# A transformer kernel with written-out queues: another order for all engines, other alternate engines, other PSUM banks

## The chip, the cores and the metric

The kernel runs on one core of a Trainium2 chip. A core has five engines with a queue each: TensorE (PE in the profile; its weight loads are listed apart as PEld), VectorE (DVE), ScalarE (ACT), GpSimd (POOL) and SyncE (SP), which here issues all DMAs. An engine takes the instructions of its queue strictly in order, and waits on semaphores for the others. The metric is the device time of one execution in microseconds (us).

## What is computed

Four layers in a row on `x` of 2048 tokens by 512 features: attention, MLP, attention, MLP, both attention layers with the same weights and both MLPs with the same weights. Cut to what matters:

```
def A(x, wqkv, wo):                      # 32 heads of 16, window of 256 tokens back
    q, k, v = split(x @ wqkv)
    scores = q @ k.T * 16 ** -0.5        # masked: 0 <= query - key < 256
    return (softmax(scores) @ v) @ wo
def B(x, w1, b1, w2, b2):                # 512 -> 1792 -> 512
    return gelu(x @ w1 + b1) @ w2 + b2
x = A_x
x = x + A(layernorm(x)); x = x + B(layernorm(x))
x = x + A(layernorm(x)); x = x + B(layernorm(x))
```

Data are bfloat16, products are accumulated in float32. `A_x` is the only input of tokens that is used.

## The kernel before

**Tiles.** Tokens are cut into 16 tiles of 128, `X` holds them in SBUF. The two passes through attention give 32 tiles and 16 blocks `b` of two tiles (blocks 0 to 7 are the first attention layer, 8 to 15 the second). The MLPs run in ten jobs (`JOBS`) of two or four tiles. Attention of block `b` needs K and V of blocks `b` and `b-1`, so the four layers overlap: while one block is in its softmax, matmuls of MLP jobs and of other blocks can run.

**One block.** `lnq` and `kv` take the layer norm of two tiles (statistics `bs`, `ba` on DVE, a power of -1/2 on POOL, the normalised `xn` on DVE), transpose it (by PE for the first tiles and the last two, else by DMA, steps `tx`), and project Q, K, V (`q`, `k`, `v`, line 653; `k` and `q` are 256 columns wide, `v` 512). The evacuations from PSUM are `qe`, `ke`, `ve`. V is also copied with its halves swapped by two DMAs a tile (`vs`). `attention(b)` then makes score steps `sc` (line 754): 10 of them for a full block, 5 for block 0 and for block 8. A score step writes four PSUM banks as two pairs, and each pair is read by one exponential of 128x1024 on ScalarE (`ex`, line 761), into `E` in SBUF. Parts of `E` are multiplied with a mask (`mk`, line 782, on DVE or POOL). Two value steps per block (`pv`, line 804) multiply `E` with V into a PSUM pair; DVE transposes it out (`od`, line 813), `rc` and `nm` normalise (line 821, on DVE or POOL), `ot` transposes back, four matmuls a tile give the output projection (`op`), and DVE adds it to `X` (`rs`, line 849).

**One MLP job.** 14 groups `m` (line 653) of four 512-column or 256-column matmuls; gelu on ScalarE, for eight groups straight from PSUM (`ge`, line 879), for six after DVE has added the bias (`gb`, line 871; `ga`, line 874). Then for each tile 14 steps `y` with W2 accumulate in one bank, POOL has prepared `X` plus bias (`xb`, line 887), and DVE adds (`ya`, line 894). In the last layer the tile is stored by a DMA (`out`).

**PSUM.** Eight banks of 128x512 float32. A group takes one bank or an even pair, holds it from its first matmul until the evacuation, and then frees it. With a score holding two pairs, the next score's banks, the value steps and all filler share what is left.

**What sets the order.** The program is a list of 3098 nodes (`_Plan.add`), each with its engine, what it reads and writes, which PSUM group it takes or frees, and for some an alternative engine. `_Plan.run` (line 393 on) then takes three written-out lists: `_ORDER` (line 167), a permutation of all nodes, from which each engine's queue is the subsequence of its nodes; `_ALT` (line 331), the nodes that run on their alternative engine; and `_BANKS` (line 343), the first bank of each of the 658 groups in the order in which they are taken. Semaphore waits are derived from the order afterwards (`_Sched.op`). Nothing else decides when something runs: no cost or due time is computed in the kernel. SP's queue is part of the order as well, so the place of each load, transpose and copy is in the list.

The node names in the text are the keys in the code; "score 4.6" is `sc4_6`, step 6 of block 4. 18 warm-up matmuls (`warm`) on zeros stand at the start.

Of the kernel before, what the change touches and what calls it, by code (L numbers as in the profile page):

```python
# [19 lines left out]
class _Sched:  # L20
# [147 lines left out]
    15, 34, 5, 0, 6, 14, 35, 7, 33, 28, 38, 29, 47, 8, 18, 23, 9, 36, 3, 26, 31, 10, 57, 37, 11, 22, 1, 40, 4, 24,  # L168
    2, 58, 59, 61, 17, 42, 62, 21, 60, 65, 41, 63, 19, 64, 68, 55, 32, 66, 107, 39, 69, 67, 20, 105, 50, 70, 3097,
    48, 30, 27, 53, 25, 106, 108, 71, 109, 49, 72, 110, 73, 16, 74, 114, 81, 75, 82, 111, 83, 84, 115, 85, 86, 116,  # L170
    112, 87, 88, 89, 113, 195, 153, 117, 127, 128, 151, 196, 129, 130, 154, 118, 152, 131, 119, 197, 155, 120, 156,
    98, 99, 100, 121, 12, 101, 90, 13, 102, 367, 91, 368, 104, 159, 92, 93, 157, 94, 103, 325, 76, 369, 199, 77,
    326, 95, 78, 200, 79, 370, 132, 80, 133, 96, 134, 135, 201, 323, 97, 203, 198, 137, 136, 158, 138, 205, 144,
    139, 202, 140, 145, 204, 141, 146, 160, 147, 122, 520, 217, 148, 123, 206, 124, 219, 143, 125, 208, 126, 46,
    218, 324, 43, 213, 209, 327, 328, 215, 166, 167, 168, 331, 169, 214, 207, 371, 176, 329, 177, 521, 373, 210,
    178, 330, 216, 179, 522, 171, 172, 180, 372, 161, 173, 211, 142, 174, 170, 56, 375, 220, 162, 376, 332, 163,
    164, 523, 175, 524, 221, 374, 377, 150, 212, 165, 149, 380, 378, 222, 188, 382, 189, 44, 190, 181, 45, 525,
    182, 381, 223, 385, 183, 224, 191, 386, 184, 384, 226, 225, 227, 54, 231, 232, 387, 379, 233, 526, 234, 383,
    333, 228, 185, 343, 388, 389, 334, 192, 229, 235, 344, 395, 194, 230, 335, 396, 345, 238, 346, 291, 390, 236,
    397, 239, 237, 347, 240, 336, 241, 348, 337, 349, 338, 242, 350, 244, 339, 243, 391, 399, 351, 401, 340, 341,  # L180
    352, 400, 245, 403, 342, 392, 402, 51, 353, 405, 52, 354, 355, 398, 356, 186, 360, 404, 357, 361, 362, 527,
    363, 393, 408, 364, 253, 409, 260, 261, 407, 254, 262, 410, 359, 413, 255, 246, 247, 415, 411, 256, 412, 257,
    248, 249, 250, 258, 414, 406, 564, 251, 273, 394, 274, 566, 263, 276, 416, 267, 268, 417, 565, 264, 270, 271,
    265, 277, 642, 285, 286, 423, 567, 418, 640, 275, 643, 528, 287, 529, 428, 272, 419, 282, 252, 283, 429, 288,
    259, 289, 641, 420, 308, 290, 309, 421, 424, 266, 310, 311, 279, 278, 644, 269, 422, 645, 284, 307, 280, 312,
    281, 313, 314, 315, 540, 425, 426, 568, 427, 541, 570, 316, 648, 542, 543, 649, 317, 569, 544, 318, 530, 531,
    319, 532, 187, 533, 572, 534, 193, 320, 574, 321, 646, 430, 431, 322, 647, 292, 573, 293, 294, 432, 577, 295,
    435, 579, 366, 576, 296, 545, 297, 436, 358, 571, 298, 433, 578, 546, 582, 434, 547, 437, 584, 548, 575, 550,
    438, 899, 551, 552, 650, 583, 553, 439, 651, 441, 652, 440, 653, 554, 900, 897, 585, 592, 654, 299, 549, 300,
    301, 593, 365, 302, 303, 304, 442, 581, 305, 594, 586, 535, 536, 898, 580, 596, 537, 306, 598, 538, 587, 901,  # L190
    539, 902, 597, 595, 600, 588, 557, 601, 660, 661, 662, 663, 599, 602, 605, 664, 558, 559, 607, 560, 655, 656,
    561, 457, 458, 606, 603, 610, 903, 657, 589, 658, 612, 904, 604, 453, 590, 459, 454, 476, 455, 477, 611, 485,
    486, 563, 609, 479, 591, 480, 482, 562, 613, 659, 470, 471, 483, 556, 905, 464, 465, 467, 478, 468, 484, 608,
    450, 460, 469, 461, 906, 451, 466, 446, 452, 447, 481, 443, 487, 448, 444, 473, 472, 462, 665, 474, 456, 614,
    666, 667, 445, 463, 615, 449, 475, 616, 684, 625, 626, 668, 617, 489, 686, 620, 618, 490, 491, 492, 685, 493,
    619, 621, 494, 669, 688, 687, 627, 690, 628, 622, 629, 495, 488, 623, 689, 496, 632, 692, 497, 694, 498, 624,
    691, 499, 500, 501, 630, 502, 693, 697, 504, 631, 505, 633, 1017, 506, 698, 507, 508, 634, 509, 1018, 510, 503,
    635, 699, 511, 702, 1019, 670, 512, 704, 700, 671, 672, 1020, 695, 673, 1021, 703, 674, 712, 696, 513, 514,
    701, 676, 714, 515, 706, 516, 517, 705, 518, 713, 519, 716, 638, 707, 717, 715, 718, 833, 720, 708, 721, 677,
    917, 1022, 918, 919, 709, 722, 920, 719, 710, 725, 921, 678, 727, 679, 680, 724, 681, 726, 730, 922, 636, 923,  # L200
    1023, 731, 912, 924, 728, 1024, 913, 723, 914, 915, 732, 729, 925, 711, 941, 637, 943, 734, 907, 908, 909, 733,
    910, 916, 926, 555, 735, 942, 639, 1025, 911, 736, 945, 934, 946, 935, 675, 737, 947, 738, 683, 949, 1026, 936,
# [763 lines left out]
```

## Time and profile before

| | us |
|---|---|
| median of 3 runs | 442.67 (442.11 to 443.06) |
| span of the profiled execution, first to last instruction | 442.4 |
| PE busy | 416.1 (94%) |
| ACT busy | 386.4 (87%) |
| DVE busy | 341.0 (77%) |
| POOL busy | 212.7 (48%) |
| mean DMA rate over the span | 53 GB/s |

The profile shows one execution; its device time is not listed apart from its span. In the rows of a stretch of time stand its bounds and length, then busy us and number of instructions of PE, PEld, DVE, ACT and POOL, the granted clock of TensorE (1.00 is full), the mean busy share of the 16 DMA engines and GB/s. In a row of waits stand the waiting engine and its line, the engine and line waited for, us in total, times, and the longest. In a row of a group, after the bar: us busy, mean ns of one, then idle us before it and what ended it. In a row of the order of time: start, us, engine, line, operation, output and inputs, count, and in brackets the idle time just before and who ended it. Matmuls are pipelined, so their durations overlap; starts give the rate.

### The profile page before, as it was taken

What the parts mean: (1) busy time and instruction counts of PE and PEld (TensorE: products, weight loads), DVE (VectorE), ACT (ScalarE), POOL (GpSimd) and SP (SyncE); (2) the same over time, 40 slices, a digit from 0 to 9 for tenths busy, and PEclk for the clock granted to TensorE, in tenths of its full rate; (3) what the DMA queues carried; (4) which work ended last, traced back from release to release, by engine and by line L of the source; (5) the groups of instructions that cost most, each with busy time, mean ns of one, the idle gap of its engine ahead of it and who ended that gap; (6) DMA issues with size and microseconds to landing.
All of it is one profiled execution on the core that took longest, in us unless ns stands there. A gap on an engine that the chain in (4) does not pass through costs nothing.

```text
span 442.4 us, 16864 instructions
## 1 busy us (share of the span) xinstructions
PE 416.1 (94%) x7523; PEld 233.2 (53%) x7593; DVE 341.0 (77%) x638; ACT 386.4 (87%) x458; POOL 212.7 (48%) x236
## 2 busy tenths in 40 slices
PE   8997999988789997999999999999999999999997
PEld 4555657544444563554455455455555464444675
DVE  7997789788785599967698868877888576746762
ACT  4997999999889999889899989999897988999533
POOL 3566344363442674711575454634728165804411
PEclk9999999999899999999999999999999999999999
DMA  7686422004101012121031021100421014003002
GB/s 234 184 209 185 87 64 45 20 10 69 39 3 25 16 34 56 28 46 24 4 65 31 1 57 26 34 20 10 69 39 20 20 39 105 14 1 81 15 0 73
DMA packets 48116, 23.25 MB, mean 53 GB/s; under 512 B 33196, under 2 KB 48044, under 8 KB 48044
## 3 DMA queue, kind: packets, MB, share of 16 engines
q1 hardware_dynamic: 48044, 22.17, 22.2%
q8 instruction: 60, 0.98, 0.9%
q14 instruction: 12, 0.10, 0.1%
HBM read 8.00 MB, written 2.10 MB: 23 GB/s over the span
## 4 chain that ended last, share of the span: by engine, by line
PE 79%; ACT 11%; DVE 6%; issue 2%; DMA 1%; DVEq 0%
PE ps L653 59%; PE ps L754 9%; PE ps L804 9%; ACT E L761 9%; DVE OD L813 1%; PE ps L539 1%; DVE stat L599 1%; DVE X L849 1%; DMA xnTB<-xn 1%; ACT gT L879 1%; ACT L879 1%; DVE KT L687 1%; DVE E L782 0%; PE ps L639 0%; ACT QT L590 0%
## 5 line engine op out<-in xcount | busy, mean ns | idle before, releaser
L761 ACT ACTIVATE E<-ps 128x1024 bf16<-128x1024 f32 x300 | 284.2, 1033 | 28.7 <-PE ps L754 28.0
L782 POOL TENSOR_TENSOR E<-E,mask 128x512 bf16<-128x512 bf16 (+2 forms) x111 | 120.9, 1106 | 91.3 <-ACT E L761 91.0
L653 PE MATMUL ps<-W_sb,gT 128*128 128x512 bf16 (+1 forms) x434 | 112.2, 373 | 3.2 <-issue 2.2
L653 PE MATMUL ps<-xnTB,W_sb 128*128 128x512 bf16 (+1 forms) x541 | 107.8, 336 | 3.4 <-issue 1.8
L653 PEld LDWEIGHTS ps<-xnTB,W_sb 128*128 128x128 bf16 x560 | 52.0, 98 | 42.9 <-issue 4.1
L653 PE MATMUL ps<-xnTA,Wqkv_sb 128*128 128x256 bf16 x512 | 70.7, 273 | 0.9 <-ACT E L761 0.4
L782 DVE TENSOR_TENSOR E<-E,mask 128x512 bf16<-128x512 bf16 (+2 forms) x125 | 60.1, 500 | 13.3 <-ACT E L761 12.9
L754 PE MATMUL ps<-QT,KT 32*128 32x128 bf16 (+3 forms) x1920 | 60.3, 231 | 9.8 <-ACT E L761 5.6
L653 PEld LDWEIGHTS ps<-W_sb,gT 128*128 128x128 bf16 x462 | 41.2, 98 | 41.1 <-issue 3.6
L754 PEld LDWEIGHTS ps<-QT,KT 32*128 32x128 bf16 x1920 | 28.5, 92 | 59.1 <-ACT E L761 34.9
L653 PEld LDWEIGHTS ps<-xnTA,Wqkv_sb 128*128 128x128 bf16 x512 | 47.4, 98 | 20.2 <-issue 2.9
L813 DVE STREAM_TRANSPOSE OD<-ps 128x1024 f32<-128x1024 f32 x32 | 39.9, 1246 | 21.3 <-PE ps L804 20.7
L887 POOL TENSOR_TENSOR Xb<-X,b2all 128x512 f32<-128x512 bf16 x32 | 37.7, 1180 | 34.3 <-DVE X L894 33.9
L879 ACT ACTIVATE gT<-ps,b1T 128x512 bf16<-128x512 f32 (+1 forms) x80 | 42.6, 609 | 9.5 <-PE ps L653 9.4
L804 PE MATMUL ps<-E,Va 64*17 64x128 bf16 (+3 forms) x1920 | 44.3, 234 | 1.9 <-issue 0.8
L821 POOL TENSOR_TENSOR Nb<-OD,Rc 128x512 bf16<-128x512 f32 x25 | 26.4, 1058 | 38.7 <-DVE Rc L817 29.8
L804 PE MATMUL ps<-E,Vs 64*17 64x128 bf16 (+3 forms) x1920 | 44.9, 234 | 0.0
L599 DVE BATCH_NORM_STATS2 stat<-X 128x6 f32<-128x512 bf16 x64 | 42.9, 679 | 0.5
L804 PEld LDWEIGHTS ps<-E,Va 64*17 64x17 bf16 x1920 | 37.2, 85 | 11.6 <-issue 9.0
L871 DVE TENSOR_SCALAR gT<-ps,b1T 128x512 bf16<-128x512 f32 (+1 forms) x60 | 36.8, 632 | 6.6 <-PE ps L653 6.2
L687 DVE TENSOR_TENSOR KT<-ps,parmask 128x1024 bf16<-128x1024 f32 x32 | 38.7, 1211 | 3.6 <-PE ps L653 3.6
L804 PEld LDWEIGHTS ps<-E,Vs 64*17 64x17 bf16 x1920 | 38.0, 85 | 0.2
(55 smaller groups left out, 348.8 us busy)
## 6 DMA issues: line engine op xcount, KB each, us to landing
Vs<-Va SPq DMA_DIRECT2D x64, 68.0 KB, 2.0
W_sb<-in_B_w_dram SPq DMA_DIRECT2D x4, 512.0 KB, 4.8
out_dram<-X SPq DMA_DIRECT2D x15, 128.0 KB, 1.8
X<-in_A_x_dram SPq DMA_DIRECT2D x3, 512.0 KB
Wqkv_sb<-in_A_wqkv_dram SPq DMA_DIRECT2D x4, 256.0 KB, 4.5
W_sb<-in_B_w_dram SPq DMA_DIRECT2D x2, 384.0 KB, 7.1
W_sb<-in_B_w_dram SPq DMA_DIRECT2D x1, 768.0 KB, 5.0
Wqkv_sb<-in_A_wqkv_dram SPq DMA_DIRECT2D x1, 512.0 KB, 6.7
```

The costliest lines, as they stand in the source:

```text
L599: add("dve", lambda e, B, t=t, k6=k6: e.bn_stats(stat6[:, k6, :], X[:, t, :]), reads=["X%d" % t], writes=["st%d" % k6], key="bs%d" % (k + j))
L653: r = e.matmul(ps[:, B[g][0], cols], lhsT, rhs, start=st, stop=sp)
L687: add("dve", lambda e, B, g=g, i=i: e.tensor_tensor(out=KT[:, kb, 2 * i : 2 * i + 2].rearrange("p c m a q -> p a (c m) q"), in0=ps[:, B[g] ...
L754: x = e.matmul(ps[:, bk[r], o : o + n], KT[rows, kb, c, m].rearrange("p a q -> p (a q)"), QT[rows, c, q : q + n], start=True, stop=True)
L761: add("act", lambda e, B, g_=g_, gi=gi: e.activation(E[:, 2 * gi : 2 * gi + 2, e0 : e0 + 512], ps[:, B[g_][0] : B[g_][0] + 2, :], AF.Exp, ...
L782: fn = lambda e, B: e.tensor_tensor(out=Ew, in0=Ew, in1=Mw, op=ALU.mult)
L804: x = e.matmul(ps[32 * r : 32 * r + VW, B[g][par], c % 2 * 2 * P + lo : c % 2 * 2 * P + hi], V[rows, (2 * b + m // 2) % VR, c * HC + 2 * r ...
L813: add("dve", lambda e, B: e.transpose(OD[:, s].rearrange("p a c q -> p (a c q)"), ps[:, B[g][0] : B[g][0] + 2, :]), reads=["ps:" + g], wri ...
L821: return e.tensor_tensor(out=Nb[:, s, :].rearrange("p (k a d) -> p a k d", a=2, d=Dh), in0=sums[:, :, :, 0:Dh], in1=rc[:, :, :, None].to_b ...
L871: add("dve", lambda e, B, g=g, fc=fc: e.tensor_scalar(out=gT[:, fc, c0 : c0 + M], in0=ps[:, B[g][0], 0:M], scalar1=b1T[:, fc : fc + 1], sc ...
L879: add("act", lambda e, B, g=g, fc=fc: e.activation(gT[:, fc, c0 : c0 + M], ps[:, B[g][0], 0:M], AF.Gelu_apprx_tanh, bias=b1T[:, fc : fc + ...
L887: add("pool", lambda e, B, t=t, xs=xs: e.tensor_tensor(out=Xb[:, xs, :], in0=X[:, t, :], in1=b2all[:], op=ALU.add), reads=["X%d" % t, "b2a ...
```

## The change

The three lists are replaced; no other line changes. The nodes, their instructions, their dependencies and the buffers in SBUF are the same.

- `_ORDER`: a new permutation. PE's queue has the same 1629 nodes; 372 of them stand more than 10 places away from where they were, most by a few places within the same stage. Three short warm-up matmuls now stand among the scores of blocks 0 and 1. Ten steps `y` more stand behind the score step 7.8, and one step `q`. The queues of ScalarE, DVE, POOL and SP are reordered likewise. SP's begins with x tiles 0, 1, 4-7, then K weights, x tiles 2-3, Q weights, the bias; before, with x tiles 0, 1, 2-3, the bias, then Q, K weights.
- `_ALT`: 164 nodes instead of 172; 104 are in both. Masks on DVE and POOL: 133 and 103 (before 125 and 111). Normalisations `nm`: 11 and 21 (before 7 and 25). Evacuations on ScalarE: 15 `qe`, 12 `ve`, 4 `te` (before 13, 10, 3). The small addition before the power: 9 on DVE, 22 on POOL (before 10, 21).
- `_BANKS`: 658 entries again; 529 groups lie in another bank than before. Pairs are at even banks in both.

ScalarE's table is switched as often as before (19 loads in each queue).

```diff
 _ORDER = [
-    15, 34, 5, 0, 6, 14, 35, 7, 33, 28, 38, 29, 47, 8, 18, 23, 9, 36, 3, 26, 31, 10, 57, 37, 11, 22, 1, 40, 4, 24,
...
-    3080, 3053, 3054, 2734, 3055, 3056, 3057, 2906, 3058, 3059, 3096, 3060, 3061, 2387, 3062, 2923, 3063,
+    34, 15, 8, 5, 35, 14, 16, 6, 42, 24, 37, 19, 17, 38, 0, 9, 21, 57, 36, 1, 28, 10, 47, 4, 58, 7, 11, 22, 61, 59,
...
+    3080, 3059, 3060, 3095, 3061, 2923, 3062, 3096, 3063,
 ]
 
 _ALT = [
-    67, 70, 75, 102, 109, 116, 121, 148, 165, 170, 185, 192, 198, 202, 211, 216, 337, 342, 370, 374, 378, 384, 389,
...
+    67, 70, 75, 113, 116, 121, 148, 165, 185, 192, 198, 202, 207, 211, 327, 337, 364, 370, 374, 378, 379, 384, 388,
...
 ]
 
 _BANKS = [
-    0, 1, 0, 1, 0, 2, 3, 2, 3, 5, 7, 0, 6, 5, 3, 2, 5, 4, 2, 4, 2, 3, 3, 5, 0, 1, 2, 6, 1, 5, 2, 4, 6, 1, 0, 2, 4, 6,
...
+    1, 0, 1, 0, 1, 0, 7, 0, 1, 0, 1, 1, 0, 7, 1, 0, 1, 7, 6, 1, 2, 3, 2, 0, 4, 3, 2, 7, 0, 2, 4, 5, 2, 6, 0, 1, 4, 2,
...
 ]
```

361 rows, old and new, of tables (_ALT, _BANKS, _ORDER) are left out of this document.

## The prediction

> **What bounds the kernel now.** I read the page first (busy shares and the slices), then the busy times in six stretches cut at score steps, then the waits, then the order of time around the worst place. A score step is the block of matmuls on line 754 that fills two PSUM pairs; ScalarE empties each pair with one exponential (line 761). I write "score 4.6" for step 6 of attention block 4.
>
> ```profile
> span 442.4 us, 16864 instructions
> PE 416.1 (94%) x7523; PEld 233.2 (53%) x7593; DVE 341.0 (77%) x638; ACT 386.4 (87%) x458; POOL 212.7 (48%) x236
> PEclk9999999999899999999999999999999999999999
> ```
> ```profile
> 0.00:10.69 10.69, 9.18 (x61) 5.36 (x62) 8.27 (x22) 5.53 (x9) 4.03 (x15) 1.00 0.77 229
> 10.69:55.72 45.03, 40.91 (x795) 26.39 (x802) 38.92 (x73) 41.48 (x54) 24.92 (x30) 1.00 0.66 167
> 55.72:81.69 25.97, 25.60 (x520) 17.74 (x523) 22.10 (x44) 24.74 (x34) 10.86 (x11) 1.00 0.26 54
> 81.69:141.85 60.16, 52.48 (x983) 27.38 (x992) 47.75 (x91) 55.27 (x63) 27.29 (x31) 0.97 0.15 25
> 141.85:204.68 62.83, 58.60 (x1187) 32.42 (x1197) 50.75 (x98) 57.81 (x65) 32.49 (x34) 1.00 0.17 34
> 204.68:440.08 235.40, 229.31 (x3987) 123.91 (x4028) 173.17 (x312) 201.60 (x237) 113.13 (x118) 1.00 0.16 34
> ```
> ```profile
> PEld ps L754 <- ACT E L761: 34.9, 80, 1.5
> ACT E L761 <- PE ps L754: 28.0, 50, 1.8
> ```
> The columns are the stretch, its length, then PE, PEld, DVE, ACT and POOL busy, the granted clock, DMA share and GB/s. The cuts are scores 0.0, 2.1, 3.0, 5.3 and 7.8. From 204.68 on PE is busy 229.31 of 235.40: nothing is left there but PE's own work, and ScalarE has 34 us to spare. Between 10.69 and 204.68 (193.99 us) PE is busy 177.59 and ScalarE 179.30. Neither is full; they wait for each other by turns, as the two wait rows say: a score waits for the exponential that frees its banks, then the exponential for the score. What a new order can win lies in these 16.4 us of idle PE, and is decided by how evenly other matmuls are laid between the scores.
>
> **The prices.**
> ```profile
> 200.25 0.81 PE L653 MATMUL ps<-xnTB,W_sb 128*128 128x512 bf16 x3
> 200.90 0.59 PE L653 MATMUL ps<-W_sb,gT 128*128 128x512 bf16 x2
> 201.33 0.82 PE L653 MATMUL ps<-xnTA,Wqkv_sb 128*128 128x256 bf16 x6
> 201.99 0.38 PE L653 MATMUL ps<-xnTB,W_sb 128*128 128x512 bf16 x1
> 204.68 0.40 PE L754 MATMUL ps<-QT,KT 32*128 32x192 bf16 x12
> 205.01 1.68 PE L653 MATMUL ps<-W_sb,gT 128*128 128x512 bf16 x7
> 206.63 0.40 PE L754 MATMUL ps<-QT,KT 32*128 32x256 bf16 x8
> ```
> ```profile
> 213.70 1.37 PE ps L804 x120
> L761 ACT ACTIVATE E<-ps 128x1024 bf16<-128x1024 f32 x300 | 284.2, 1033 | 28.7 <-PE ps L754 28.0
> L590 ACT ACTIVATE QT<-ps 128x512 bf16<-128x512 f32 x13 | 8.0, 613 | 1.6 <-PE ps L653 1.6
> ```
> Starts, not durations, give PE's rate: a 512-column matmul takes (200.90 - 200.25)/3 = 0.217, a 256-column one (201.99 - 201.33)/6 = 0.11, a score 205.01 - 204.68 = 0.33, and from 205.01 to 206.63 seven matmuls and the wait for the score take 1.62, so each score adds 0.10. A value step (line 804) takes 1.37. An exponential takes 284.2/300 = 0.95 in sequence (I use 0.94), a copy on ScalarE 0.61. Six fillers and a score are 1.64 + 0.10 against 1.88 for two exponentials: seven fillers match ScalarE, fewer leave PE waiting, more leave ScalarE waiting.
>
> **The change, part by part.**
>
> *Filler between scores.* With these prices I added, for each score step, the PE work since the score before and the ScalarE work up to its second exponential, and took the larger. In the list of before PE's work in the four stretches is 40.7, 25.8, 51.1 and 58.8, ScalarE's 43.1, 25.7, 55.7 and 58.2, and the larger parts sum to 45.4, 27.7, 60.2 and 63.7, together 197.0; the trace has 193.99, so the sum describes this kernel within 2%. In the new list PE has 41.5, 24.7, 51.1 and 56.9, ScalarE 41.9, 25.7, 55.1 and 58.8, and the larger parts sum to 44.3, 26.7, 57.6 and 63.9, together 192.5. That is 4.5 less. But the new list has laid ten steps of the second MLP product and a little more behind score 7.8, 2.3 us of PE work, where PE is the bound: net -2.2. That is one end. The other: were the eight banks deep enough to even out everything inside a stretch, only the larger total of each stretch would count, 183.4 before and 181.5 after: -1.9 + 2.3 = +0.4. The measured 193.99 lies 78% of the way from 183.4 to 197.0, so I take -2.2 + 0.22 x 2.6 = -1.6.
>
> *The hole at 113 us, and the clock.*
> ```profile
> 112.73 0.40 PE L754 MATMUL ps<-QT,KT 32*128 32x256 bf16 x8
> 114.38 0.40 PE L754 MATMUL ps<-QT,KT 32*128 32x256 bf16 x8 [1.25 <-ACT E L761]
> 116.21 0.40 PE L754 MATMUL ps<-QT,KT 32*128 32x192 bf16 x12 [0.46 <-ACT E L761]
> 116.79 2.32 PE ps L804 x125
> 121.30 1.02 ACT L761 ACTIVATE E<-ps 128x1024 bf16<-128x1024 f32 x1 [1.78 <-PE ps L754]
> ```
> ```profile
> 37.98:41.39 3.41, 2.03 (x29) 1.24 (x31) 2.50 (x3) 3.04 (x4) 1.02 (x1) 1.00 0.40 77
> 113.07:116.48 3.41, 1.70 (x32) 1.02 (x28) 3.08 (x7) 3.41 (x5) 0.26 (x1) 1.00 0.20 40
> 116.48:119.89 3.41, 2.90 (x138) 2.15 (x132) 0.70 (x1) 3.02 (x4) 1.21 (x2) 0.50 0.20 42
> ```
> Scores 4.5 (112.73) and 4.6 (114.38) have nothing between them. In the 3.41 us up to 116.48 PE is busy 1.70, and for the next 3.41 its clock is 0.50: the value step takes 2.32 where 1.37 is normal, and ScalarE stands for 1.78. The new list has five matmul steps ahead of score 4.6 and a value step ahead of 4.7, so this hole is closed. I price the lost half clock at 2.32 - 1.37 = 0.95 (ends: 0, if another hole takes its place, and 1.78) and take -0.95. [...]
>
> *The start.*
> ```profile
> 0.78 1.35 SPq L548 DMA_DIRECT2D X<-in_A_x_dram  x3
> X<-in_A_x_dram SPq DMA_DIRECT2D x1, 256.0 KB, 2.9
> 6.00:7.00 1.00, 1.00 (x8) 0.46 (x6) 0.97 (x2) 0.91 (x2) 0.00 (x0) 1.00 1.15 342
> 5.69 1.28 DVE L599 BATCH_NORM_STATS2 stat<-X 128x6 f32<-128x512 bf16 x2
> 9.40 1.22 DVE L687 TENSOR_TENSOR KT<-ps,parmask 128x1024 bf16<-128x1024 f32 x1 [0.38 <-PE ps L653]
> ```
> On SP's queue the 256 KB load of x tiles 2 and 3 goes from third to fifth, behind 512 KB (tiles 4 to 7) and 256 KB of weights. At 342 GB/s these 768 KB are 2.3 us, so it lands near 7 instead of 1.7 + 2.9 = 4.6, and the statistics move from 5.69 to about 7.1. In the new DVE queue two more statistics (0.68 each, in the fence below) and both normalisations of that pair stand ahead of the first K evacuation, which goes from 9.40 to about 10.8: score 0.0 comes up to 1.35 later. But those two statistics (2 x 0.68 = 1.36) are then done, and DVE, busy 38.92 of the next 45.03, has them off its list. Ends 0 and +1.35; I take +0.5, nearer to the work than to the wait.
>
> *Engines exchanged.*
> ```profile
> L782 POOL TENSOR_TENSOR E<-E,mask 128x512 bf16<-128x512 bf16 (+2 forms) x111 | 120.9, 1106 | 91.3 <-ACT E L761 91.0
> L782 DVE TENSOR_TENSOR E<-E,mask 128x512 bf16<-128x512 bf16 (+2 forms) x125 | 60.1, 500 | 13.3 <-ACT E L761 12.9
> L821 POOL TENSOR_TENSOR Nb<-OD,Rc 128x512 bf16<-128x512 f32 x25 | 26.4, 1058 | 38.7 <-DVE Rc L817 29.8
> L599 DVE BATCH_NORM_STATS2 stat<-X 128x6 f32<-128x512 bf16 x64 | 42.9, 679 | 0.5
> ```
> Masks go from 111 to 103 on POOL, normalisations from 25 to 21, and ScalarE makes five more evacuations: POOL loses 8 x 1.1 + 4 x 1.06 = 13 us of 212.7; ScalarE gets 5 x 0.61 = 3.1, all of it behind 204.68, where it has 34 to spare; DVE gets 8 x 0.5 and four normalisations (0.75 each, an estimate at the rate of its other 512-wide work) and gives up five evacuations of 0.68 (estimated alike), about +3.5 of 341.0. I cost them at nothing: the cover is DVE's 12.4 idle us of 60.16 in the stretch where it gets most of it. Were that gone, up to +3.5.
>
> *The other DMAs, the tail.* The first two transposes for the MLP still follow all three W1 loads, with about as many bytes ahead; 0, with 0.5 either way. Behind the last score both lists hold PE work alone (29.6 and 30.3 us, inside the 2.3 above); the last output tile is the same: 0.
>
> Sum: -1.6 - 0.95 + 0.5 = -2.05. The profiled span is 442.4 and the median of the runs 442.67, so 0.27 lies outside the span or between executions; I leave it there: 442.67 - 2.05 = 440.6. Measurement tells this kernel from no change at about 0.2%, 0.9 us.
>
> **The rivals.**
>
> *Not faster: work pushed behind 204.68 is not bought back.* If ScalarE idles in the first stretches as it does now (193.99 - 179.30 = 14.7), score 7.8 comes only by its lower work sooner, 182.7 - 181.5 = 1.2, and then 2.3 us more PE work follows: +1.1, 443.8. For it: the two wait rows are a mutual lock that even filler need not loosen. Against: the sum of larger parts followed the trace. It decides as soon as less than 2.3 us are won before score 7.8.
>
> *Another hole halves the clock.* The new list has its emptiest place at scores 4.2 and 4.3: 0.33 + (0.33 + 4 x 0.217) = 1.53 of PE work in four exponentials, 3.76. The rows put the limit between 1.70 and 2.03 busy in 3.41, so if a window falls there, the 0.95 is paid as now: 441.6. [...]
>
> *Nothing moves.* The first score is late by the full 1.35, the mutual waits give -1.6, and a half clock is paid in some other place: 442.4, within 0.2%. For it: 768 KB stand ahead of x tiles 2 and 3. Against: DVE has work to put in the gap.
>
> **How the numbers follow.** Forecast 440.6: 0.38. Second hole 441.6: 0.14. No change: 0.18. Slower, 443.8: 0.30. Faster is the first two, 0.52. The likeliest one's own range is 439.0 (442.67 - 2.2 - 0.95 with no cost at the start is 439.5, less 0.5 from the other DMAs) to 441.6. The whole range goes from 437.8, 1.2 below that for stalls the sum does not count, to 444.4, the slower rival with half of the start's cost.
>
> **What would show it.** Score 7.8 should start near 200.3 (204.68 + 0.5 - 0.95 - 1.6 - 2.3) and the rest take 2.3 longer. Right: fewer than 80 waits of scores for exponentials, clock 1.00 around 105 to 125. Wrong: first score later than 12, score 7.8 after 202.4, a half-clock slice elsewhere, or PE idle above 6 us after score 7.8.

## The result: 3% slower, and the profile after

The changed kernel takes 455.96 us (455.68 to 456.53) beside 442.49 us (442.11 to 443.06) for the kernel before: 1.0308 times as long, 95% interval 1.0293 to 1.0323. The forecast was 440.6, the range 437.8 to 444.4. In this kernel's code every line number is 7 lower than before (the score is line 747, its exponential 754, the matmul helper 646, the value step 797); in the experiments' kernels numbers can be one higher again.

The page after, and the same six stretches cut at scores 0.0, 2.1, 3.0, 5.3 and 7.8:

```profile
span 454.1 us, 16925 instructions
...
PE 428.3 (94%) x7593; PEld 232.9 (51%) x7593; DVE 346.4 (76%) x644; ACT 389.6 (86%) x463; POOL 202.2 (45%) x225
...
PEclk9989999999899999899999999999999999999999
```
```profile
0.00:12.32 12.32, 9.19 (x57) 5.07 (x59) 9.02 (x22) 6.07 (x10) 4.20 (x16) 1.00 0.87 258
12.32:62.36 50.04, 44.13 (x814) 28.04 (x814) 40.40 (x76) 40.81 (x53) 26.98 (x30) 0.97 0.59 138
62.36:87.20 24.84, 24.84 (x509) 16.25 (x508) 21.89 (x41) 23.81 (x33) 11.22 (x10) 1.00 0.17 29
87.20:147.67 60.47, 53.91 (x996) 26.51 (x990) 49.08 (x94) 55.39 (x63) 23.18 (x28) 0.97 0.19 33
147.67:211.74 64.07, 59.21 (x1190) 31.66 (x1191) 51.63 (x94) 56.41 (x64) 32.76 (x35) 0.97 0.21 34
211.74:451.60 239.86, 237.03 (x4041) 125.39 (x4040) 174.17 (x321) 207.14 (x245) 103.85 (x108) 1.00 0.17 33
```

PE's busy times of before and after can't be subtracted: the profile of before holds 7523 of the 7593 matmuls, this one all. So the 416.1 of before is too low and the idle time that the prediction read from it too high. A kernel below that differs from before in two pieces alone, with all 7593 recorded, has PE busy 424.4 of the same span of 442.4; between its scores 0.0 and 7.8 PE idles 12.6, where the prediction read 16.4.

The waits, as the profile puts them down:

```profile
ACT E L754 <- PE ps L747: 32.4, 47, 3.3
PEld ps L747 <- ACT E L754: 30.9, 76, 1.1
...
PE ps L646 <- DMA xnTA<-xn: 4.5, 2, 2.6
...
PE ps L646 <- DMA xnTB<-xn: 3.2, 2, 2.3
...
PE ps L797 <- DMA Vs<-Va: 1.4, 1, 1.4
```

Scores wait a little less for exponentials (34.9 to 30.9), exponentials a little more for scores (28.0 to 32.4). New are PE's own waits for DMAs: before, the longest was 0.7. Four of them in the order of time, the last with the two issues that precede it on SP's queue:

```profile
26.28 2.13 PE L646 MATMUL ps<-xnTA,Wqkv_sb 128*128 128x256 bf16 x10 [2.62 <-DMA xnTA<-xn]
...
57.92 0.60 PE L646 MATMUL ps<-xnTA,Wqkv_sb 128*128 128x256 bf16 x4 [1.86 <-DMA xnTA<-xn]
...
127.17 0.81 PE L646 MATMUL ps<-xnTB,W_sb 128*128 128x512 bf16 x3 [2.27 <-DMA xnTB<-xn]
...
324.36 1.27 SPq L625 DMA_TRANSPOSE xnTB<-xn  x1
325.67 0.59 SPq L695 DMA_DIRECT2D Vs<-Va  x1
...
327.84 0.28 PE L797 MATMUL ps<-E,Va 64*17 64x256 bf16 x4 [1.36 <-DMA Vs<-Va]
```

The last is a V copy (`vs24_0`, one half of tile 24's swapped V). Its source was ready at 313.35, but it was issued at 325.67, because other steps stand ahead of it in SP's order, and landed 2 us later: the value step stood.

The wait rows miss cases in which the weight load ahead of a matmul did the waiting. So for every stretch of over 0.3 us in which PE stood, from 6 us on, I took the operands and bank releases that the next matmul needs and asked which came last. In us:

| what ended PE's idle time | before | after |
|---|---|---|
| ScalarE (exponentials, which free the scores' banks) | 6.2 | 2.8 |
| VectorE | 2.7 | 4.5 |
| the landing of a DMA | 0.6 | 11.8 |
| sum | 9.5 | 19.1 |

So the new order did loosen the waits it was predicted to loosen, by 3.4, and pays 11.2 for transfers that land too late. The sum rises by 9.6. By stretch, with the differences that the prediction's "larger parts" gave:

| stretch, up to score | predicted | measured | new waits for landings in it |
|---|---|---|---|
| 0.0 | +0.5 | +1.6 | 0.8 (first weights) |
| 2.1 | -1.1 | +5.0 | 2.6, 1.9 (transposes 4, 9), 1.1 (V copy 2) |
| 3.0 | -1.0 | -1.1 | none |
| 5.3 | -2.6 | +0.3 | 2.3 (transpose 39), 0.9 (V copy 7) |
| 7.8 | +0.2 | +1.2 | 0.9 (transpose 42) |
| end | +2.3 | +4.5 | 1.4 (V copy 24) |

In the one stretch without a late transfer the working is right to 0.1. That is a weak test, since by the prediction's own sums this stretch has 1.1 less of PE's work (25.8 to 24.7) and would be shorter by it in any case. The rest of the time is TensorE's clock: three windows at half clock, each behind a window in which PE was busy 0.71, 1.51 and 1.67 of 3.41.

```profile
23.10:26.51 3.41, 0.71 (x22) 0.33 (x11) 1.53 (x3) 2.60 (x3) 1.06 (x2) 1.00 0.37 78
26.51:29.92 3.41, 3.41 (x23) 1.91 (x21) 2.45 (x6) 0.91 (x1) 0.00 (x0) 0.50 0.86 267
111.84:115.25 3.41, 1.51 (x24) 0.46 (x16) 3.31 (x5) 3.07 (x4) 2.07 (x2) 1.00 0.54 86
115.25:118.66 3.41, 3.41 (x23) 1.05 (x26) 2.26 (x6) 2.75 (x3) 1.78 (x2) 0.50 0.43 76
180.11:183.52 3.41, 1.67 (x36) 0.60 (x34) 3.08 (x6) 3.41 (x4) 1.83 (x3) 1.00 0.46 77
183.52:186.93 3.41, 2.86 (x7) 0.89 (x7) 1.77 (x4) 2.03 (x3) 1.56 (x2) 0.50 0.45 92
```

A run's time is its span plus 1.8 us (454.1 and 455.93 here). The kernel before was run again 30 times: 27 runs at a granted clock of 0.999 or 1.00 have spans of 439.7 to 441.7, median 440.5, and three at 0.996 have 441.8 to 442.2. The profiled execution of 442.4, with its half-clock window at 116.48, is thus nearly 2 us slower than the usual one, and a window costs some 1.4. The account is then 9.6 of waits and three windows at 1.3, together 13.5, where the medians differ by 13.5. The 1.3 is chosen to close it, and lies beside the 1.4.

### The profile page after: what moved, and what is told of

It reads as the page before. It is cut to its first block, busy times and chain, and to the rows that moved or that the text cites. A ratio compares the mean times of both kernels' runs of the same rounds, so it can differ in the third digit from the quotient of the medians.

```text
span 454.1 us, 16925 instructions
## 1 busy us (share of the span) xinstructions
PE 428.3 (94%) x7593; PEld 232.9 (51%) x7593; DVE 346.4 (76%) x644; ACT 389.6 (86%) x463; POOL 202.2 (45%) x225
## 4 chain that ended last, share of the span: by engine, by line
PE 73%; ACT 9%; DMA 7%; DVE 7%; SPq 3%; issue 1%; POOL 0%; DVEq 0%
PE ps L646 57%; PE ps L747 8%; PE ps L797 8%; ACT E L754 7%; DMA xnTB<-xn 3%; DMA xnTA<-xn 2%; DVE E L775 2%; DVE stat L592 1%; DMA X<-in_A_x_dram 1%; SPq L695 1%; SPq L625 1%; DVE X L887 1%; ACT gT L872 1%; DVE X L842 1%; DVE Va L581 1%
## 5 line engine op out<-in xcount | busy, mean ns | idle before, releaser
L754 ACT ACTIVATE E<-ps 128x1024 bf16<-128x1024 f32 x300 | 284.4, 1036 | 33.7 <-PE ps L747 32.4
L775 POOL TENSOR_TENSOR E<-E,mask 128x512 bf16<-128x512 bf16 (+2 forms) x103 | 111.6, 1095 | 96.0 <-ACT E L754 95.8
L646 PE MATMUL ps<-xnTB,W_sb 128*128 128x512 bf16 (+1 forms) x560 | 115.7, 340 | 3.3 <-DMA xnTB<-xn 3.2
L646 PE MATMUL ps<-W_sb,gT 128*128 128x512 bf16 (+1 forms) x462 | 118.8, 374 | 0.0
L646 PE MATMUL ps<-xnTA,Wqkv_sb 128*128 128x256 bf16 x512 | 74.2, 277 | 5.5 <-DMA xnTA<-xn 4.5
L775 DVE TENSOR_TENSOR E<-E,mask 128x512 bf16<-128x512 bf16 (+2 forms) x133 | 65.3, 512 | 10.6 <-ACT E L754 10.2
L747 PEld LDWEIGHTS ps<-QT,KT 32*128 32x128 bf16 x1920 | 28.2, 93 | 54.8 <-ACT E L754 30.9
L797 PE MATMUL ps<-E,Va 64*17 64x128 bf16 (+3 forms) x1920 | 43.3, 230 | 5.8 <-DVE Va L581 1.6
L797 PE MATMUL ps<-E,Vs 64*17 64x128 bf16 (+3 forms) x1920 | 43.9, 230 | 0.0
L814 POOL TENSOR_TENSOR Nb<-OD,Rc 128x512 bf16<-128x512 f32 x21 | 22.5, 1072 | 43.6 <-DVE Rc L810 43.6
L646 PE MATMUL ps<-Wo_sb,OT 128*128 128x512 bf16 x128 | 40.6, 388 | 0.2 <-DVE OT L820 0.2
```

The lines of the kernel that those rows point to most:

```text
L646: r = e.matmul(ps[:, B[g][0], cols], lhsT, rhs, start=st, stop=sp)
L747: x = e.matmul(ps[:, bk[r], o : o + n], KT[rows, kb, c, m].rearrange("p a q -> p (a q)"), QT[rows, c, q : q + n], start=True, stop=True)
L754: add("act", lambda e, B, g_=g_, gi=gi: e.activation(E[:, 2 * gi : 2 * gi + 2, e0 : e0 + 512], ps[:, B[g_][0] : B[g_][0] + 2, :], AF.Exp, ...
L775: fn = lambda e, B: e.tensor_tensor(out=Ew, in0=Ew, in1=Mw, op=ALU.mult)
L797: x = e.matmul(ps[32 * r : 32 * r + VW, B[g][par], c % 2 * 2 * P + lo : c % 2 * 2 * P + hi], V[rows, (2 * b + m // 2) % VR, c * HC + 2 * r ...
L814: return e.tensor_tensor(out=Nb[:, s, :].rearrange("p (k a d) -> p a k d", a=2, d=Dh), in0=sums[:, :, :, 0:Dh], in1=rc[:, :, :, None].to_b ...
```

## The experiments

In the diffs OLD and NEW are the node lists of the kernel before and of the changed kernel. No experiment leaves any of the computation out; one makes a score step three times. Score times are starts, compared with the profiled execution of before.

### Which of the three lists

**New order and engines, other banks.** 500 of the 658 groups lie elsewhere, each chosen by how long a bank had been free.

```diff
 _BANKS = [
-    1, 0, 1, 0, 1, 0, 7, 0, 1, 0, 1, 1, 0, 7, 1, 0, 1, 7, 6, 1, 2, 3, 2, 0, 4, 3, 2, 7, 0, 2, 4, 5, 2, 6, 0, 1, 4, 2,
+    0, 1, 2, 3, 4, 5, 6, 7, 0, 1, 2, 3, 4, 5, 6, 0, 7, 1, 5, 2, 3, 6, 4, 0, 2, 7, 6, 4, 0, 2, 7, 6, 2, 4, 0, 1, 2, 6,
...
```

> The new order and the new alternate engines with another set of PSUM banks: 500 of 658 groups get another bank, chosen so that each takes the bank that has been free longest. If the banks cause the loss, the time moves by several us, toward 444 to 450. If late transfers and the start cause it, the banks are innocent: 456 within 1.5, the gaps of PE near 24, 58, 114 and 127 us stand where they were, and score 1.1 starts at 28.3 within 0.5.

Measured 462.31 (460.52 to 464.1), ratio 1.0447. PE's waits for exponentials rise from 2.8 to 9.3. The banks of the change are better than these by 6 us. This is outside both ranges, and score 1.1 comes at 25.18 and not at 28.3, so neither theory is confirmed; one worse set does not show that the banks of the change cost nothing. It gives no sign that they do.

**New order and banks, the engines of before.**

```diff
 _ALT = [
-    67, 70, 75, 113, 116, 121, 148, 165, 185, 192, 198, 202, 207, 211, 327, 337, 364, 370, 374, 378, 379, 384, 388,
+    67, 70, 75, 102, 109, 116, 121, 148, 165, 170, 185, 192, 198, 202, 211, 216, 337, 342, 370, 374, 378, 384, 389,
...
```

> The new order and the new banks with the 128 engine choices of the kernel before. If the exchanged engines cause the loss, most of the 13.5 us goes: 443 to 447. If late transfers cause it, only the start gains: the second V evacuation runs on ScalarE again, the four V copies leave about 2 us sooner and the first transposes behind them too, score 1.1 near 26.5, and the end 453 to 455. If only the late x tiles cause it: 456 within 1.

Measured 470.99 (470.14 to 471.85), ratio 1.0643: 15 worse than the change. None of the three ranges holds. Up to score 9.1 it stays within 3.0 of the change, then falls behind steadily, and VectorE is busy 357.7 for the 638 operations that took 341.0 before. With the new order the new engine choices are a gain and not the loss. That makes the order the first suspect.

### Where along the order

**The first 344 nodes (through score 1.9) from before, the rest new.** In this kernel and the next, nodes and groups keep the engines and banks of the list that they come from.

```diff
-_ORDER = NEW
+_ORDER = OLD[:344] + [n for n in NEW if n not in OLD[:344]]
```

> Order, engines and banks of the kernel before up to score 1.9 (344 of some 3100 steps), the new ones behind it. If the loss is a sum of local stalls, the 4.7 us of the start are won and no more: 451.3 within 1. If a late start only delays transfers whose lateness then grows by itself, more comes back: 447 or less. [...]

Measured 452.22 (451.7 to 452.75), ratio 1.0219. At score 2.3 it is 0.9 ahead of before; at 5.0 it is 2.5 behind, at 6.8 3.8, at 9.9 5.0, at 12.6 6.3. The loss has many places; the list up to score 1.9 makes 3.7 of it (455.96 - 452.22).

**Before through score 8.0, new behind.**

```diff
-_ORDER = OLD
+_ORDER = OLD[:1456] + [n for n in NEW if n not in OLD[:1456]]
```

> The list of before through score 8.0 (1456 of 3098 steps, with sets that differ from the new list's by 3 steps), the new one behind it; no bank is changed. In the mixed list that changed at score 1.9 the lag on before grew from 4.2 us at score 8.0 to 7.8 at the end. If the new list's second half loses by its own order, the end is at 446 (442.6 + 3.6). If it loses only because it starts late, or only through work that was pushed behind score 7.8, the end is 442.6 to 443.5.

Measured 446.55 (446.17 to 447.16), ratio 1.0097. PE in the order of time; the first two rows are at the seam of the two lists:

```profile
207.81 0.41 PE L748 MATMUL ps<-QT,KT 32*128 32x128 bf16 x24 [1.68 <-ACT E L755]
210.18 0.40 PE L748 MATMUL ps<-QT,KT 32*128 32x192 bf16 x12 [0.57 <-DVE X L888]
...
318.95 0.28 PE L798 MATMUL ps<-E,Va 64*17 64x256 bf16 x4 [1.01 <-DMA Vs<-Va]
...
377.57 0.28 PE L798 MATMUL ps<-E,Va 64*17 64x256 bf16 x4 [0.46 <-DVE E L776]
```

From score 8.0 on PE is busy 232.80; with the list of before (in the next kernel) 232.53. The work is the same; the 3.5 us by which this part is longer (239.6 beside 236.06) are these four waits, 3.7 in all. The two at the seam, 2.25 together, belong to the joining of the lists, so the new list's own loss here is the other 1.5. The kernel also shows the front part of before without a half-clock window: from score 4.7 to 4.8 it takes 3.45, in the profiled execution of before 4.64.

**Before with two pieces of the new order, scores 1.9 to 2.6 and 4.2 to 5.1.**

```diff
-_ORDER = OLD
+_ORDER = []
+for L, n in ((OLD, 344), (NEW, 528), (OLD, 801), (NEW, 913), (OLD, 3098)):
+    _ORDER += [i for i in L[:n] if i not in _ORDER]
```

> The list of before with two pieces of the new one: between scores 1.9 and 2.6, where the mixed list won 1.1 us on before, and between scores 4.2 and 5.1, where the new list has no hole at score 4.6. If gains are local: 440.6 to 441.5, and no half clock at 116. [...] If a piece drags stalls behind it: 443 or more.

Measured 444.86 (443.95 to 446.33), ratio 1.0058, interval 1.0039 to 1.0077. Compared with the kernel just shown, which has the list of before here and no half clock either, score 2.6 comes 0.96 earlier, as the larger parts had it, but 2.9 comes 0.73 later. Over the second piece it catches up to 0.1 behind at score 5.0, and is 1.2 behind at 5.3. What a piece of the new order wins is real but small, and isn't kept; why, is argued only: the list behind it was not made for the earlier arrival.

### The start

**New order, the loads in before's order** on SP's queue (eleven moved; the diff shows the first).

```diff
 _ORDER = [      # SP's nodes
-    34, 35, 42, 37, 38, 36, 47, 40,
+    34, 35, 38, 47, 36, 37, 40, 42,
...
```

> The new order with the initial loads alone in the order of the kernel before (x tiles 2 and 3 third). If the late x tiles start the loss, score 0.0 comes at 10.7 and score 1.1 near 24 to 25 instead of 28.3, with no half clock near 27; the end at 451 to 452.5. If the first evacuations and copies on DVE and SP's queue are the cause, score 0.0 comes at 10.7 and score 1.1 still at 26.7 or later: 454.3. If later work takes it all up: 456.

Measured 455.41 (453.53 to 457.29), ratio 1.0291: two runs, 3.8 apart, which show no change. Score 0.0 starts at 12.89, later still than the 12.32 of the change. The reason stands on VectorE's queue, where two statistics of x tiles 6 and 7 come ahead of the first K evacuation and wait for that load. First this kernel, then the change:

```profile
9.78 1.29 DVE L593 BATCH_NORM_STATS2 stat<-X 128x6 f32<-128x512 bf16 x2 [2.66 <-DMA X<-in_A_x_dram]
```
```profile
7.66 1.28 DVE L592 BATCH_NORM_STATS2 stat<-X 128x6 f32<-128x512 bf16 x2 [1.95 <-DMA X<-in_A_x_dram]
...
11.04 1.22 DVE L680 TENSOR_TENSOR KT<-ps,parmask 128x1024 bf16<-128x1024 f32 x1
```

**The same, and those two statistics (nodes 323, 325) behind the K evacuation (85).**

```diff
 _ORDER = [
-    323, 82, 109, 32, 71, 110, 72, 325, 73, 83, 3097, 74, 114, 84, 111, 75, 86, 115, 85, 26, 112, 116, 87, 88, 89,
+    82, 109, 32, 71, 110, 72, 73, 83, 3097, 74, 114, 84, 111, 75, 86, 115, 85, 323, 325, 26, 112, 116, 87, 88, 89,
...
```

> The new list with the initial loads in the order of before, and with the statistics of x tiles 6 and 7 moved on DVE's queue from ahead of the normalisations of tiles 2 and 3 to behind the first K evacuation. If that place on DVE's queue, behind the second x load, holds score 0.0, it comes at 10.7 to 11.1 (with the loads alone it came at 12.9). If the start decides what follows, score 1.1 comes by 24.3 and the end near 453; if the landing of the first transposes decides, score 1.1 stays at 25.5 or later and the end at 455.

Measured 453.46 (451.62 to 456.82), ratio 1.0263. Score 0.0 now starts at 10.86, 0.17 from before: this was the start's loss. But score 2.4 is still 2.2 behind before and the whole run 11 slower: PE then waits for the output weights, transpose 6 and V copy 2.

### The clock

**Before with score 4.6 made three times**, so that PE has work where it stood for the exponential ahead of the half clock.

```diff
-                    for c, m, kb, q, o, n in pieces:
+                    for c, m, kb, q, o, n in pieces * (3 if (b, g) == (4, 6) else 1):
```

> The kernel before with the matmuls of score 4.6 issued three times over, the same values into the same banks: 0.66 us more PE work in the hole at 114. If the share of busy time in the 3.41 us ahead decides on the clock (1.70 there, 2.36 now), the half clock at 116 is gone and the end comes 0.95 earlier, 441.7. If the gaps decide, the half clock stays: 442.6 to 443. If ScalarE is what bounds this place, the clock is whole and the time stays at 442.6.

Measured 449.61 (447.45 to 451.0), ratio 1.016. The window is full clock again, and another one isn't:

```profile
113.07:116.48 3.41, 2.11 (x42) 1.32 (x40) 3.13 (x7) 3.38 (x5) 0.93 (x2) 1.00 0.17 35
179.80:183.21 3.41, 1.50 (x97) 0.96 (x76) 2.34 (x4) 0.05 (x1) 1.98 (x3) 1.00 0.22 48
183.21:186.62 3.41, 3.41 (x9) 1.22 (x10) 0.75 (x1) 1.94 (x2) 1.36 (x2) 0.50 0.02 5
```

Score 4.8 comes at 122.00, not earlier than the 120.85 of before, and between scores 7.1 and 7.2 3.9 us are lost: PE stands 1.91 in the middle of a score, for nothing that the profile shows, and the half clock follows.

```profile
182.92 0.28 PE L748 MATMUL ps<-QT,KT 32*128 32x256 bf16 x2 [1.91 <-issue]
```

Closing the hole at 113 wins nothing here, and before's usual runs (clock 1.00) say that there is mostly nothing to win. The stall of 1.91 I can't explain. All four runs are 5 to 8.5 us slower than before, the one at clock 1.00 too (447.45), so it is no accident of one execution, and the kernel is a poor measure of anything behind 180.

### The transfers

**The change with eight transfers moved forward on SP's queue**: V copies 2, 3, 7, 24 and 25 and transposes 8 and 9. All other queues, and the banks, are the change's.

```diff
 _ORDER = [      # SP's nodes
...
-    143, 43, 54, 149,
+    143, 142, 149, 43, 54,
...
-    45, 142, 245, 243, 56,
+    45, 245, 243, 527, 529, 56,
...
-    440, 904, 906, 365,
+    440, 365, 904, 906,
...
-    2049, 1955, 2395, 2043, 2397, 2050, 2124, 2126, 2042,
+    2049, 2043, 2042, 1955, 2395, 2050, 2397, 2124, 2126,
...
```

> The new list with eight DMAs moved forward on SP's queue alone, every other queue, engine and bank as in the new list: V copies 2 and 3 ahead of the load of Wo, transposes 8 and 9 ahead of the V copies and loads that they stood behind, V copies 7, 24 and 25 ahead of transposes and an output that waited for their data. If late landings cause the loss, PE's waits at 39.6 (1.08), 56.1 (1.86), 100.4 (0.87) and 326.5 (1.36) go and the end comes 5 us earlier, near 451; at least 3 us earlier, 453. If other waits take their place, it stays at 455 to 456.

Measured 452.91 (451.91 to 455.76), ratio 1.0257: 3.05 less than the change. The waits at V copies 2, 7 and 24 and at transpose 9, 5.2 together, are gone; left are PE's

```profile
25.87 1.26 PE L647 MATMUL ps<-xnTA,Wqkv_sb 128*128 128x256 bf16 x10 [2.35 <-DMA xnTA<-xn]
...
35.95 0.61 PE L647 MATMUL ps<-xnTA,Wqkv_sb 128*128 128x256 bf16 x4 [0.92 <-DMA xnTA<-xn]
```

and 2.0 at transpose 39; waits for landings fall from 11.8 to 7.3. The second row is new: transpose 6 landed 6.3 us after its issue, in the change 5.2. The gain isn't the clock's: at a granted clock of 0.989 this kernel takes 452.91, the change at 0.988 takes 455.68 to 455.99. So late landings do cost time, and part of the gain is lost to the next one. Transposes 4, 6 and 39 stay late here.

**The same with the load of x tiles 2 and 3 third and the two statistics behind the K evacuation.**

```diff
 _ORDER = [      # SP's nodes
-    34, 35, 42, 37, 38, 36,
+    34, 35, 38, 42, 37, 36,
...
 _ORDER = [      # VectorE's nodes
-    106, 108, 323, 325, 114, 111, 85,
+    106, 108, 114, 111, 85, 323, 325,
...
```

> The same, and the load of x tiles 2 and 3 third instead of fifth, with the statistics of tiles 6 and 7 behind the first K evacuation on DVE. If stalls add up: score 0.0 at 10.7 to 11.1 and 1.3 us less than the kernel with SP's queue alone, near 449.5. If the start is given back: the same time as that kernel.

Measured 453.94 (452.75 to 453.95), ratio 1.0258: nothing won. Score 0.0 comes at 11.14, but PE then arrives earlier at transpose 4, waits the more, and a window at half clock (0.50) follows at 26.64:

```profile
26.38 2.10 PE L647 MATMUL ps<-xnTA,Wqkv_sb 128*128 128x256 bf16 x10 [2.61 <-DMA xnTA<-xn]
```

**The other way round: before with V copies 2 and 24 (nodes 142, 2042) moved back on SP's queue**, behind steps like those that stand ahead of them in the new order.

```diff
 _ORDER = [      # SP's nodes
...
-    330, 142, 56,
+    330, 56,
...
-    54, 194,
+    54, 142, 194,
...
-    2124, 2042, 2049,
+    2124, 2049,
...
-    2397, 2169,
+    2397, 2042, 2169,
...
```

> The kernel before with two V copies moved back on SP's queue, nothing else: copy 2 behind three weight loads (it landed 6.5 us ahead of its use, and should now land 4 us behind it) and copy 24 behind two transposes of tiles 53 and 29 (4.5 us ahead, now 2 us behind). If landings on SP's queue decide, PE waits at value step 1.0 and at value step 12.0 and the end is 446 to 449. If the order of before has slack for it: 442.5 to 443.5.

Measured 447.17 (446.46 to 448.62), ratio 1.0119: two late transfers cost the kernel before 4.8 us by the medians, and 4.1 between runs at a clock of 1.00 (446.46, the profiled one, and 442.39).

```profile
38.18 0.28 PE L798 MATMUL ps<-E,Va 64*17 64x256 bf16 x4 [3.25 <-DMA Vs<-Va]
...
319.45 0.28 PE L798 MATMUL ps<-E,Va 64*17 64x256 bf16 x4 [1.46 <-DMA Vs<-Va]
```

Their sum is 4.7. Most of a late landing is thus paid: measured against the kernels above that hold the same list with its transfers in place, the first wait has become a lag of 2.7 at score 3.9 and 2.3 at 7.8, while the second stays 1.5 to the end.

**An order that leaves more room for every landing.** From the kernel with the first 344 nodes of before, the nodes behind are moved so that transfers are issued earlier or used later (on PE's queue 549, VectorE's 233, ScalarE's 70, GpSimd's 75, SP's 61); and, as a control, before's list moved in the same manner (487, 229, 69, 76, 57).

```diff
 _ORDER = [
...
-    407, 254, 262, 410, 359, 413, 255, 528, 187, 256, 257, 258, 263, 264, 414, 411, 246, 247, 265, 412, 273, 248,
+    407, 254, 262, 406, 255, 365, 410, 413, 414, 263, 264, 265, 256, 257, 258, 273, 411, 246, 247, 248, 187, 415,
...
```

> The mixed list (before through score 1.9, the new list behind it, 452.2 us) with some 900 of its steps moved by up to some tens of places behind score 1.9, engines and banks as they were. The moves were chosen by adding up this case's durations with every transpose landing 1.7 us and every V copy 1.4 us later than their fastest, and DVE and GpSimd a little slower, so that PE waits for nothing even then. If too little slack for landings and for DVE is what the new list loses by, its waits for DMAs (6.1 us in the mixed list) go and the end is 438 to 442. If the loss lies in something that this sum doesn't hold, 447 or more.

```diff
 _ORDER = [
...
-    407, 254, 262, 410, 359, 413, 255, 246, 247, 415, 411, 256, 412, 257, 248, 249, 250, 258, 414, 406, 564, 251,
+    407, 254, 262, 406, 528, 187, 410, 365, 366, 255, 413, 415, 529, 414, 246, 247, 248, 249, 250, 251, 256, 257,
...
```

> The list of before, moved in the same way behind score 1.9 (some 900 steps). If slack is what counts, its waits (9.5 us in all, 1.1 of them for DMAs) shrink to some 6 and the end is 438 to 440.5. If ScalarE and PE hold each other as before: 442 to 443. If the new order meets delays that the sum doesn't hold, as the new list did: 444 or more.

Measured 458.14 (456.94 to 459.15), ratio 1.0355, and 464.28 (463.29 to 464.61), ratio 1.049. PE's waits for landings did fall, to 0.7 (from 6.1) and to none over 0.3; but those for VectorE rise to 14.7 and 18.7. The pages' busy times, the order with room first:

```profile
PE 419.0 (92%) x7524; PEld 231.8 (51%) x7593; DVE 370.3 (81%) x644; ACT 392.2 (86%) x464; POOL 203.5 (45%) x224
```
```profile
PE 422.0 (91%) x7524; PEld 232.8 (50%) x7593; DVE 376.0 (81%) x638; ACT 389.6 (84%) x458; POOL 216.3 (47%) x236
```

The control does the 638 VectorE operations of before, with the same tiles, in 376.0 instead of 341.0. So the mended order failed. By the expectations above, both runs speak for a loss that a sum of landings doesn't hold, and a question is left: what makes VectorE's operations longer? It is the masks and the layer norm's `xn`; first `xn` before, then the control's masks and `xn` (the masks of before, 60.1 and 500, stand in the prediction). They make 18 and 10 of the 35 us; the residual additions keep their length (679 and 675 ns).

```profile
L627 DVE TENSOR_SCALAR xn<-X,statmv,rstd 128x512 bf16<-128x512 bf16 x64 | 26.6, 431 | 3.2 <-POOL rstd L617 1.6 <-issue 1.2 <-DVE E L782 0.3
```
```profile
L776 DVE TENSOR_TENSOR E<-E,mask 128x512 bf16<-128x512 bf16 (+2 forms) x125 | 78.4, 653 | 8.6 <-ACT E L755 8.4
L621 DVE TENSOR_SCALAR xn<-X,statmv,rstd 128x512 bf16<-128x512 bf16 x64 | 36.9, 588 | 6.9 <-POOL rstd L611 5.2
```

### VectorE beside GpSimd

In the change this happens ahead of PE's wait at 174.49. VectorE, GpSimd and PE in the order of time:

```profile
170.50 4.49 POOL L775 TENSOR_TENSOR E<-E,mask 128x512 bf16<-128x512 bf16 x4
...
173.36 2.04 DVE L775 TENSOR_TENSOR E<-E,mask 128x768 bf16<-128x768 bf16 x1
...
175.33 0.68 DVE L842 TENSOR_TENSOR X<-X,ps 128x512 bf16<-128x512 bf16 x1
...
176.06 1.04 PE L646 MATMUL ps<-Wqkv_sb,xnTA 128*128 128x512 bf16 x4 [1.57 <-DVE X L842]
...
178.13 0.28 PE L797 MATMUL ps<-E,Va 64*17 64x256 bf16 x4 [0.71 <-DVE Va L581]
```

The mask of score 6.4 on VectorE takes 2.04, where a mask takes 0.51 on average. It ends at 175.40, 0.41 after GpSimd's masks (170.50 + 4.49 = 174.99). Behind it on the queue the residual addition of tile 10 is late, and PE with it.

**The change with that mask (node 1340) behind the residual addition (1121).**

```diff
 _ORDER = [
...
-    1312, 1120, 1340, 1313, 1314, 1121, 1339,
+    1312, 1120, 1313, 1314, 1121, 1340, 1339,
...
```

> The changed kernel with one instruction moved: VectorE's half of the mask of score 6.4 goes behind the residual addition of tile 10 in the list, and so on VectorE's queue; nothing else moves, no bank changes. In the changed kernel that mask took 2.04 us at 173.36 while GpSimd's mask of the same score ran, where masks of its size elsewhere take about 0.55; the residual addition behind it came late, and TensorE waited 1.58 at 174.5 and 0.71 at 177.4. Theory 1 (the mask is held by GpSimd's operation and holds the queue): both waits go, score 6.6 to 7.2 come 1.5 to 2.3 us earlier, and 453.7 to 454.7 us in all if nothing behind takes it back. Theory 2 (the addition was late by its own operands, or the mask was long by itself): the wait of about 1.5 stays, 455.6 to 456.5. Under both, value step 6.0 may wait for the mask instead, up to 0.7.

Measured 453.85 (453.41 to 454.46), ratio 1.0264, interval 1.0239 to 1.0289: 2.1 less than the change.

```profile
170.06 5.12 POOL L776 TENSOR_TENSOR E<-E,mask 128x256 bf16<-128x256 bf16 x5
...
173.93 0.69 DVE L843 TENSOR_TENSOR X<-X,ps 128x512 bf16<-128x512 bf16 x1 [0.32 <-PE ps L647]
174.54 1.05 DVE L776 TENSOR_TENSOR E<-E,mask 128x768 bf16<-128x768 bf16 x1
...
177.66 0.28 PE L798 MATMUL ps<-E,Va 64*17 64x256 bf16 x4 [1.18 <-DVE Va L582]
```

The addition comes 1.4 earlier and PE's wait of 1.57 is gone. The mask now takes 1.05 and again ends 0.41 after GpSimd's (175.18): it was held, and is itself short. The second wait did not go; value step 6.0 waits 1.18 for a V evacuation. So the mask itself is worth less than 2.1: from score 6.4 to 6.9 this kernel gains 0.66 on the change, and a further 1.7 by score 7.2, where the change has its half clock at 183.52 and this kernel has none (its three are at 38.16, 113.26 and 126.91). Two kernels above with the mask in its old place have no half clock there either (the other banks, and the eight transfers with the start), so whether the mask or the windows' place decides it stays open.

**Both: the eight transfers and the mask.** The two edits above together.

> The changed kernel with eight transfers moved forward on the transfer queue (as in the kernel that read 452.9) and the mask of score 6.4 moved as well. If losses of different places add up: 1.5 to 2.3 below the kernel with the transfers alone, 450.6 to 451.4. If what one edit wins the list takes back at its next point where both engines meet: within 0.6 of 452.9. Waits of TensorE above 1 us left: transpose 4, transpose 6 and transpose 39 only.

Measured 450.71 (449.71 to 453.28), ratio 1.0198: 5.25 less than the change, where the edits alone won 3.05 and 2.1. The gains add up. Beside the kernel with the transfers alone, scores 6.4 to 6.9 again gain 0.65, and the step to 7.2 another 1.5, where that kernel has a half clock at 181.80. Waits above 1 us that are left are transposes 6 (3.6) and 39 (2.3), as expected, but also score 4.2 (2.2), value step 6.0 (1.2) and 1.5 at 58.97 in the middle of an MLP group, for nothing that the profile shows; transpose 4 has none this time.

None of these beats the kernel before.

## Why the prediction was wrong, step by step

Three of its four signs of being wrong came: the first score at 12.32, score 7.8 after 202.4, and half clocks elsewhere.

**"The other DMAs, the tail": 0, with 0.5 either way. This step failed.** It counted bytes ahead of the first two MLP transposes and looked at no other transfer. Measured: +11.2 of waits for landings in eight places, one of them (0.8) at the start. The order that moves PE's work also moves the place of 78 steps on SP's queue and the time at which PE asks for each tile. What was needed is, for each transfer, its use less its issue, against the spread of landings; the trace of before had the row for that (rows for the transposes into `xnTA`, in before and after):

```profile
DMA to landing us min/median/max: 2.4/3.3/5.5
```
```profile
DMA to landing us min/median/max: 2.4/3.2/5.2
```

The landings of these transposes are no slower after than before. Of the V copies one is: copy 2, issued behind three weight loads, landed after 8.3, where the slowest before took 5.9. From issue to use, as they ran, 7 of the 122 transposes and V copies leave less than 1 us over the quickest landing (2.4 and 1.9) after, and 2 before. PE's waits count as room in this, so the count is a weak sign: the three largest waits, at transposes 4, 39 and 9, are not among the 7, and it is still 7 with the eight transfers moved. What shows the step wrong are the moves on SP's queue alone and back again: -3.05, and +4.1 at the same clock, for a term put at 0. For the rest of the 11.2 the waits are measured, but no experiment moves those transfers forward alone.

**"Filler between scores": -1.6.** Right in direction: PE's idle time that ScalarE ended fell by 3.4, and the waits of scores that I asked for, fewer than 80, are 76. As a sign this was useless, since what PE waits for next isn't in that row. Its size isn't tested: score 7.8 came at 211.74 and not near 200.3, and the -1.1 for -1.0 in the stretch without a late transfer is as much PE's work. The 16.4 us of idle PE that it starts from are partly missing records.

**"The hole at 113 us, and the clock": -0.95.** Void. The median of before does not pay such a window (27 of 30 runs), so closing it wins nothing. I had set the profiled span beside the median and put 0.27 outside the span; it is 1.8, and the profiled execution was slow by nearly 2. The new order does close that hole, but has three others; the one at 115.25 follows the wait at score 4.2, the place that the second rival named. All half-clock windows shown are 3.41 long. In the change they begin 26 and 20 times 3.413 apart (26.51, 115.25, 183.52), and from run to run at another place (116.48, 115.25, 183.21 and 26.64 are not a multiple of 3.41 apart). The windows shown that led to a half clock had PE busy 0.71, 1.50, 1.51 and 1.67 of 3.41, and no wait longer than 2.62. The limit that the prediction read from two rows, between 1.70 and 2.03 busy, doesn't hold. In the kernel with both edits two windows in a row, from 31.47, have 1.51 and 1.74 busy and the clock stays full; in the one with the two statistics moved, a window with 1.91 (up to 181.05) is followed by a half clock. What decides between 1.5 and 1.9 stays open.

**"The start": +0.5, ends 0 and +1.35.** Measured +1.63, above the end. The statistics were named, but their wait for the load, 1.95, was not: the load of x tiles 4 to 7 and not only that of 2 and 3 had to land first. Moving the load and the statistics back made the change 453.46 in three scattered runs (451.62 to 456.82), and on top of the eight transfers it won nothing, with transpose 4 late as before.

**"Engines exchanged": 0.** Taken alone they are worth 15 us to the new order. The cover, VectorE's idle time, was of the wrong kind: what counted at the place shown was which VectorE operation met a GpSimd one (the mask of score 6.4 took 2.04). That cost 0.65 directly, and 2.1 with what follows it.

**The tail and the slower rival.** "2.3 us PE work pushed behind score 7.8" is there: the last stretch is 4.5 longer, which is 2.3 and the two waits of 1.36 (V copy 24) and 0.78 (a mask). The rival had the sign right for a cause that makes up a sixth of the loss; that is luck.

Not settled: what makes one landing slow. The first eight transposes stand in the same order in the change and in the kernel with the mask moved, yet transpose 4 took 4.5 and 2.5, transpose 6 5.2 and 8.3.

## What to carry to other kernels

Before reordering queues, write down for each transfer the time from issue to use, and hold it against the largest landing that any run at hand shows, not the median (here 8.3 beside 3.4); a transfer behind other steps on an in-order queue has the issue time of its queue, not of its data (here 325.67 and not 313.35). A gain in the wait that bounds a kernel is kept only if what PE meets next is there as early (here 3.4 was won and 11.2 lost). And compare the profiled execution with the median by several spans before a term is priced from one event in it.

## What was not expected of the hardware

- **A VectorE mask that ends with GpSimd's masks.** The VectorE mask of score 6.4, which starts while GpSimd works, ends 0.41 after GpSimd's operation in both kernels shown (175.40 after 174.99; 175.59 after 175.18), whatever is left of that: it takes 2.04 and 1.05 us, where masks of its shape have a median of 0.55. Over the control above, masks are busy 18 us longer than before (60.1 to 78.4). Whether each of those was held in the same way is not shown, and why `xn` is longer too (431 to 588 ns) no run here separates.
- **Landings of one and the same transfer differ between runs** (transpose 6: 5.2 in the change, 8.3 with the mask moved alone). The transposes into `xnTA`, in the kernel with the mask moved alone, against 5.2 at most in the change:

```profile
DMA to landing us min/median/max: 2.4/3.4/8.3
```

- **A half clock behind a window in which PE was busy 0.71 to 1.91 of 3.41**, as listed above, at a place that moves from run to run, and not behind every such window (1.51 and 1.74); so a profile can have three of them (the change) or none (the kernel with two pieces of the new order).
